# More zero products in the opening chain of an attention and feed-forward kernel, and the last pair of token blocks stored in the ordinary way

## The chip, the cores and the metric

The kernel runs on one core of one Trainium2 chip. The metric is the device time of one execution in microseconds (us). Before the change it is 247.01 us, the median of 8 runs that lie between 246.40 and 247.34 us. Lower is better.

The engines are named as in the profile: PE (TensorE, products), PEld (its weight loads), DVE (VectorE), ACT (ScalarE), POOL (GpSimd) and SP (SyncE, which here only issues transfers). A "q" behind a name (SPq, ACTq) means the engine's instruction queue rather than its arithmetic.

## The reference

For 8 batches, 8 heads, 576 positions and a head width of 64, a 32-slot memory attention is computed and fed to a bilinear feed-forward layer:

```
a      = softmax over the 32 slots of phi
k_m    = a^T k          v_m = a^T v          (32 x 64 per head)
attn   = softmax(q k_m^T / 8)                (576 x 32 per head)
x      = attn v_m, heads put side by side    (4608 x 512)
result = ((x @ w_a) * (x @ w_b)) @ w_out     (512 -> 1536 -> 512)
```

Inputs and result are float32; the kernel computes in float16 with float32 sums.

## The kernel before, in words

**Work per batch.** A batch goes through named units (a dictionary `us[b]` of closures, lines 187 to 382). The ones that matter here: `exp0`, `exp1` take the exponential of phi on ACT (L195); `ks`/`vs` sum k and v under those weights on PE (L256), with a reciprocal and a scaling on DVE (L265, L266); `kt`/`vt` transpose the sums on PE (L274), copied out by DVE (L277); `qt` transposes q on DVE (L204); `s` makes scores on PE (L292); `e` takes their exponential on ACT (L305); `den` sums them on PE (L314), with a logarithm on ACT (L315); `nr` normalises on ACT and DVE (L323, L325). Then `v..`/`hv..` fold v_m into the weights w_a and w_b on PE (L337), and `x..`/`hx..` copy the folded weights out of PSUM on ACT and DVE (L349). A fold needs its columns of w_a or w_b in SBUF: `hv0` columns 0 to 255, `hv1` 256 to 511, `v1` 512 to 1023, `v2` 1024 to 1535; `a` stands for w_a and `b` for w_b.

**Up and down.** `up` (L584) multiplies the attention by the folded weights, one block of 128 feed-forward columns at a time: `pa` (L592), copied by ACT (L595), `pb` (L602), and their product on DVE (L605) into `ht`. `down` multiplies `ht` by w_out, first singly (L389), later for two token blocks at a time in seven products of half size, as Strassen's method does (`two_downs`, L453; its products are L462).

**Loads.** All weights and most inputs are cast from float32 to float16 by transfers that POOL issues in the order of the code (L111 to L176). The order is q, k and v of batch 0, then w_a and w_b in the column pieces named above (`load_wab`, L98 to L100), then w_out in thirds, mixed with batch 1.

**The opening.** PE runs 16 products of a zeroed tile (`fill`, L147; `cols` is the width, 512 in this first call and 256 in the chain). Then `chain(0, ...)` (L671) calls the units of batch 0 in the written order; an entry `f2` in that list is `fill(2, 256)`, two zero products whose result nobody reads. Each `fill` takes one PSUM bank from a list in which the longest unused bank is first (`Banks`, L122). Then `ups` (L672 to L674) runs the first twelve `up` blocks with the folds put between them by an explicit list, one entry after each `pa` and each `pb`. PE does all this in program order. For batch 0 the order is: `hv0a`, `pa` of block 0, `hv0b`, `pb`, `hv1a`, block 1 with `hv1b` behind it, block 2, `v1a`, block 3, `v1b`, blocks 4 and 5, `pa` of block 6, `v2a`, `v2b`, the rest.

**The end.** `two_downs` makes two output tiles of 128 tokens by 512 columns, `o1` and `o2`, in four quarters, in this order: right half of `o1`, right half of `o2`, left half of `o1` (each a DVE addition, L473), left half of `o2` (a scaling). `store` (L447) issues two transfers per tile, one for each 64 tokens. Elsewhere in the kernel a whole tile is stored by two transfers of 128 KB on SP as soon as its last quarter is there. For the last pair (`ends`, L458) each half tile is stored by itself, two transfers of 64 KB each: right `o1` on POOL, POOL (L492); right `o2` on SP, ACT (L498); left `o1` on SP, ACT (L506); left `o2` on SP, ACT (L518). There the last quarter is scaled by DVE (L514) instead of ACT (L516).

Of the kernel before, what the change touches and what calls it, by code (L numbers as in the profile page):

```python
# [11 lines left out]
ALU = mybir.AluOpType  # L12
# [6 lines left out]
def kernel(  # L19
# [11 lines left out]
    nc = tc.nc  # L31
# [3 lines left out]
    d_model, d_ff = moe_w_a.shape  # L35
# [111 lines left out]
    def fill(n, cols=512):  # L147

        pw = banks.tile([P, 512], F32, name="pw")
        for _ in range(n):  # L150
            nc.tensor.matmul(pw[:, :cols], warm[:, :P], warm[:, :cols], start=True, stop=True)
# [267 lines left out]
    NH = d_model // 2  # L419
    w_sums = wpool.tile([P, 4, KH, NH], F16, name="w_sums")  # L420

    def quarter(x, y):
        return wo_sb[:, KH * x:KH * (x + 1), NH * y:NH * (y + 1)]
# [7 lines left out]
    def tokens_of(cidx, x):  # L431
        pair, c = divmod(cidx, NI)
        return ht[:, KH * x:KH * (x + 1), P * c:P * (c + 1)]
# [13 lines left out]
    def store(o_sb, cidx, cs=slice(0, d_model), engines=(nc.sync, nc.sync)):  # L447
        pair, c = divmod(cidx, NI)
        for z in range(2):
            slot = 2 * c + z  # L450
            engines[z].dma_start(out=out_rows[2 * pair + slot // NI, slot % NI, :, cs], in_=o_sb[64 * z:64 * z + 64, cs])

    def two_downs(self, cidx):  # L453
        S1, S2, S4, S3 = (h_sums[cidx][:, x] for x in range(4))
        T1, T2, T3, T4 = (w_sums[:, x] for x in range(4))
        (a11, a12), (a21, a22) = ([tokens_of(cidx + y, x) for x in range(2)] for y in range(2))
        scale = 1.0 / (CS * CS)
        ends = cidx == PAIRED[-1]  # L458

        def products(po, lhs, rhs, first=False):  # L460
            for i in range(KH):
                nc.tensor.matmul(po, lhs[:, i], rhs[:, i], start=first and i == 0,  # L462
                                 stop=i == KH - 1, skip_group_check=not first)
                if i < KH - 1:
                    yield

        def part(po, name):
            x = ppool.tile([P, NH], F32, name=name)
            nc.scalar.mul(out=x, in_=po, mul=scale)  # L469
            return x  # L470

        def plus(o, po, x):
            nc.vector.scalar_tensor_tensor(out=o, in0=po, scalar=scale, in1=x, op0=ALU.mult, op1=ALU.add)  # L473

        o1, o2 = (opool.tile([P, d_model], F32, name="o_sb") for _ in range(2))
        y, ybank = banks.take([P, NH], F32, "py", hold=True)
        yield from products(y, a11, quarter(0, 0), True)
        u1 = part(y, "u1")
        yield
        v, vbank = banks.take([P, NH], F32, "pv", hold=True)  # L480
        self.brim = True
        yield from products(v, S1, T1, True)
        u5 = part(v, "u5")
        yield
        yield from products(y, S2, T2)
        u2 = part(y, "u2")
        yield
        yield from products(v, S4, quarter(1, 1))
        banks.free(vbank)
        plus(o1[:, NH:], v, u2)  # L490
        if ends:
            store(o1, cidx, slice(NH, d_model), (nc.gpsimd, nc.gpsimd))  # L492
        self.brim = False
        yield
        yield from products(y, S3, T3)
        plus(o2[:, NH:], y, u5)
        if ends:
            store(o2, cidx + 1, slice(NH, d_model), (nc.sync, nc.scalar))  # L498
        yield
        x, xbank = banks.take([P, NH], F32, "px", hold=True)  # L500
        self.brim = True
        yield from products(x, a12, quarter(1, 0), True)
        banks.free(xbank)
        plus(o1[:, :NH], x, u1)
        if ends:
            store(o1, cidx, slice(0, NH), (nc.sync, nc.scalar))  # L506
        else:
            store(o1, cidx)
        self.brim = False
        yield  # L510
        yield from products(y, a22, T4)
        banks.free(ybank)
        if ends:
            nc.vector.tensor_scalar(out=o2[:, :NH], in0=y, scalar1=scale, scalar2=None, op0=ALU.mult)  # L514
        else:
            nc.scalar.mul(out=o2[:, :NH], in_=y, mul=scale)  # L516
        if ends:
            store(o2, cidx + 1, slice(0, NH), (nc.sync, nc.scalar))  # L518
        else:
            store(o2, cidx + 1)  # L520
        yield
# [5 lines left out]
    class Work:  # L527
# [10 lines left out]
        def products(self):  # L538
            for cidx in PAIRED:
                yield from two_downs(self, cidx)  # L540
# [67 lines left out]
    def ups(steps, side=()):  # L608

        side = iter(side)  # L610
        for step in steps:
            for _ in up(*step):
                work.advance()
                next(side, us[step[0]]["-"])()
        for f in side:
            work.advance()
            f()

    def steps(b, lo, hi):

        return [(b, i, (0, 1)) for i in range(lo, hi)]
# [14 lines left out]
    def slots(b, names):  # L636

        def both(fs):
            return lambda: [f() for f in fs]
        def unit(n):  # L640
            if n == "fin":
                return lambda: work.pull(-work.done % NFF)
            if n == "L":
                return lambda: load(b + 2) if b + 2 < B else None
            if n[0] == "y":
                return lambda: some(int(n[1:]))
            if n[0] == "d" and n[1:].isdigit():
                return lambda: work.pull(int(n[1:]))
            return us[b + n.endswith("'") - n.endswith("_")][n.rstrip("'_")]

        return [both([unit(n) for n in x.split("+")]) for x in names.split()]
# [3 lines left out]
    def some(n):  # L655
        for _ in range(n):
            next(early, None)

    def chain(b, plan):


        for x in plan.split():
            if x[0] == "f":
                fill(int(x[1:]), 256)
            elif x[0] == "y":
                some(int(x[1:]))
            else:
                us[b][x]()

    fill(16)  # L670
    chain(0, "exp0 exp1 ks0 kt0 qt0 qt1 f2 s0 e0 ks1 kt1 den0 qt2 qt3 f2 s1 nr0 e1 vs0 vs1 den1 vt0 vt1 nr10 nr11 hv0a hx0a")  # L671
    ups(steps(0, 0, 4), slots(0, "hv0b+hx0b hv1a+hx1a - hv1b+hx1b - v1a+x1a - v1b+x1b"))  # L672
    load(2)
    ups(steps(0, 4, 12), slots(0, "- - - - v2a+x2a+v2b+x2b - -"))  # L674
# [48 lines left out]
```

The softmax here doesn't subtract the row's maximum and nothing guards it: scores larger than these inputs give would overflow.

## Time and profile before

| what | value |
|---|---|
| median of 8 runs | 247.01 us |
| the profiled execution's own time | 247.07 us |
| its span (first to last instruction) | 245.3 us |
| PE busy | 231.8 us, 94% of the span |
| PEld, DVE, ACT, POOL busy | 67%, 69%, 64%, 63% |
| granted PE clock, mean | 0.986 |
| chain that ended last: PE, transfers | 82%, 11% |
| `pw` zero products in the chain | 4, of 256 columns |

The profile is a page of one execution and a trace that can be asked for more. Its start times are microseconds from the first instruction. A line of a timeline gives the start, the length, the engine, the source line, the operation with output and inputs, the number of instructions merged into the line, and in brackets the idle time of that engine before it with what ended it. The start of a transfer is its issue; "to landing" counts from there to the moment at which its semaphore tells that the data have arrived. The granted clock (PEclk) is a share of full speed. The lengths of products overlap: 128x288 products start 0.12 us apart at a clock of 1, though each is listed with some 0.29 us.

### The profile page before, as it was taken

What the parts mean: (1) busy time and instruction counts of PE and PEld (TensorE: products, weight loads), DVE (VectorE), ACT (ScalarE), POOL (GpSimd) and SP (SyncE); (2) the same over time, 40 slices, a digit from 0 to 9 for tenths busy, and PEclk for the clock granted to TensorE, in tenths of its full rate; (3) what the DMA queues carried; (4) which work ended last, traced back from release to release, by engine and by line L of the source; (5) the groups of instructions that cost most, each with busy time, mean ns of one, the idle gap of its engine ahead of it and who ended that gap; (6) DMA issues with size and microseconds to landing.
All of it is one profiled execution on the core that took longest, in us unless ns stands there. A gap on an engine that the chain in (4) does not pass through costs nothing.

```text
span 245.3 us, 7629 instructions
## 1 busy us (share of the span) xinstructions
PE 231.8 (94%) x3016; PEld 165.2 (67%) x3016; DVE 168.9 (69%) x406; ACT 158.2 (64%) x409; POOL 153.9 (63%) x126
## 2 busy tenths in 40 slices
PE   7569999999998999999999999999999999999993
PEld 2234574456655857777787777877787877888882
DVE  3454794477959958876995549866996576756742
ACT  2364772678697489578855858577856867565330
POOL 8734263499799028892798769892849177937001
PEclk9995999999999999999999999999999999999999
DMA  6999999999969803983059832597030303032154
GB/s 203 208 197 207 207 256 207 256 217 285 224 179 208 173 2 104 230 142 88 16 130 226 194 86 43 153 198 172 21 68 3 86 3 87 4 87 55 43 128 119
DMA packets 26099, 33.81 MB, mean 138 GB/s; under 512 B 1968, under 2 KB 20528, under 8 KB 26064
## 3 DMA queue, kind: packets, MB, share of 16 engines
q0 software_dynamic: 19344, 22.84, 50.9%
q1 hardware_dynamic: 6208, 9.70, 15.9%
q10 hardware_dynamic: 512, 0.79, 0.9%
q8 instruction: 23, 0.38, 0.6%
q14 instruction: 12, 0.10, 0.1%
HBM read 42.47 MB, written 9.44 MB: 212 GB/s over the span
## 4 chain that ended last, share of the span: by engine, by line
PE 82%; DMA 11%; DVE 3%; issue 1%; ACT 1%; POOL 1%; DVEq 0%; POOLq 0%
PE pa L592 19%; PE pb L602 18%; PE py L462 16%; PE pv L462 8%; DMA wb_sb<-in_moe_w_b_dram 7%; PE pva L337 5%; PE po L389 5%; DMA kv_sb<-in_v_dram 4%; PE px L462 4%; PE pkv L213 2%; PE pD L314 2%; PE pscore L292 1%; PE pT L242 1%; PE pk L256 1%; POOL q_sb L90 1%
## 5 line engine op out<-in xcount | busy, mean ns | idle before, releaser
L605 DVE TENSOR_TENSOR ht<-a_sb,pb 128x288 f16<-128x288 f16 x192 | 83.0, 449 | 42.1 <-ACT a_sb L595 28.7
L595 ACT CAST a_sb<-pa 128x288 f16<-128x288 f32 x192 | 75.1, 405 | 31.7 <-PE pa L592 29.3
L592 PE MATMUL pa<-A,vab 128*128 128x288 f16 x384 | 77.7, 292 | 1.5 <-DVE A L325 1.1
L602 PE MATMUL pb<-A,vab 128*128 128x288 f16 x384 | 77.3, 290 | 0.7 <-ACT vab L349 0.5
L444 POOL TENSOR_TENSOR h_sums<-ht 128x768 f16<-128x768 f16 x28 | 45.8, 1639 | 38.9 <-DVE ht L605 37.3
L602 PEld LDWEIGHTS <-vab 128*128 128x128 f16 x384 | 37.6, 99 | 13.5 <-issue 1.7
L592 PEld LDWEIGHTS <-vab 128*128 128x128 f16 x384 | 34.9, 99 | 16.0 <-issue 8.7
L462 PEld LDWEIGHTS <-h_sums 128*128 128x128 f16 x384 | 37.4, 98 | 6.9 <-issue 0.4
L349 ACT CAST vab<-pva 128x512 f16<-128x512 f32 (+1 forms) x52 | 28.0, 559 | 12.8 <-PE pva L337 12.8
L349 DVE CAST vab<-pva 128x512 f16<-128x512 f32 (+1 forms) x52 | 32.6, 644 | 2.8 <-PE pva L337 2.2
L462 PEld LDWEIGHTS <-ht 128*128 128x128 f16 x288 | 28.2, 98 | 5.6 <-issue 0.4
L462 PE MATMUL py<-w_sums,h_sums 128*128 128x256 f16 x192 | 30.3, 272 | 0.0
L444 POOL TENSOR_TENSOR h_sums<-h_sums,ht 128x768 f16<-128x768 f16 x14 | 23.1, 1649 | 0.9
L444 POOL TENSOR_TENSOR h_sums<-ht,h_sums 128x768 f16<-128x768 f16 x14 | 23.0, 1640 | 1.0
L305 ACT ACTIVATE E<-pscore 128x288 f16<-128x288 f32 x32 | 11.4, 417 | 11.3 <-PE pscore L292 11.2
L325 POOL TENSOR_TENSOR A<-E,R 128x576 f16<-128x576 f16 x10 | 12.7, 1275 | 7.0 <-ACT R L323 6.7
L462 PE MATMUL py<-wo_sb,ht 128*128 128x256 f16 x96 | 16.0, 273 | 0.0
L462 PE MATMUL pv<-w_sums,h_sums 128*128 128x256 f16 x96 | 16.0, 273 | 0.0
L469 ACT ACTIVATE u<-py 128x256 f32<-128x256 f32 x32 | 12.4, 387 | 5.2 <-PE py L462 5.0
L462 PE MATMUL py<-w_sums,ht 128*128 128x256 f16 x96 | 15.5, 272 | 0.1
L462 PE MATMUL px<-wo_sb,ht 128*128 128x256 f16 x96 | 15.4, 273 | 0.0
L204 DVE STREAM_TRANSPOSE qT<-q_sb 128x288 f32<-128x288 f32 x32 | 14.3, 462 | 0.6 <-DMA q_sb<-in_q_dram 0.6
(64 smaller groups left out, 261.1 us busy)
## 6 DMA issues: line engine op xcount, KB each, us to landing
out_dram<-o_sb SPq DMA_DIRECT2D x68, 128.0 KB, 2.8
kv_sb<-in_v_dram POOLq DMA_DIRECT2D x7, 576.0 KB, 10.3
phi_sb<-in_phi_dram POOLq DMA_DIRECT2D x7, 576.0 KB, 4.6
kv_sb<-in_k_dram POOLq DMA_DIRECT2D x7, 576.0 KB, 8.8
q_sb<-in_q_dram POOLq DMA_DIRECT2D x6, 576.0 KB, 13.3
wo_sb<-in_moe_w_out_dram POOLq DMA_DIRECT2D x3, 512.0 KB, 16.3
q_sb<-in_q_dram POOLq DMA_DIRECT2D x4, 288.0 KB, 12.6
wa_sb<-in_moe_w_a_dram POOLq DMA_DIRECT2D x2, 512.0 KB, 14.9
```

Of the source, the lines that this page charges most:

```text
L204: nc.vector.transpose(out=t["qT"][:, hp, :].bitcast(F32), in_=qs[b][:, hp, :].bitcast(F32))
L325: engine.tensor_tensor(out=attn[b][:, g, sl], in0=t["E"][:, g, sl], in1=t["R", g][:, sl], op=ALU.mult)
L337: nc.tensor.matmul(t["pva", lo, z][g][0][32 * j:32 * j + 32, 0:hi - lo], t["kvT"][64 * r:64 * r + 64, 4 + g, M * j:M * j + M], w_sbs[z][64 ...
L349: engine_copy(out=vabs[b][z][:, g, lo:hi], in_=pva[:, 0:hi - lo])
L389: nc.tensor.matmul(po, ht[:, i, P * c:P * (c + 1)], wo_sb[:, i, :], start=(i == 0), stop=(i == NFF - 1))
L444: engine.tensor_tensor(out=out, in0=in0, in1=in1, op=op)
L462: nc.tensor.matmul(po, lhs[:, i], rhs[:, i], start=first and i == 0, stop=i == KH - 1, skip_group_check=not first)
L469: nc.scalar.mul(out=x, in_=po, mul=scale)
L592: nc.tensor.matmul(pa, vab[0][:, g, fs], A[:, g, HALF * hf:HALF * (hf + 1)], start=(g == 0), stop=(g == 1))
L595: nc.scalar.copy(out=a_sb, in_=pa)
L602: nc.tensor.matmul(pb, vab[1][:, g, fs], A[:, g, HALF * hf:HALF * (hf + 1)], start=(g == 0), stop=(g == 1))
L605: nc.vector.tensor_tensor(out=ht[:, i, t0:t0 + HALF], in0=a_sbs[hf - hfs[0]], in1=pb, op=ALU.mult)
```

## The change

Two edits. In the last pair, the stores change: right `o1` is no longer stored by itself; right `o2` goes to SP, SP; `o1` is stored as a whole tile on SP, SP; left `o2` still goes to SP, ACT, and is scaled by ACT. In the chain of batch 0 the two entries `f2` become `f7` and `f5`, and eight further `f` entries are put in: 57 zero products of 256 columns in place of 4.

```diff
         plus(o1[:, NH:], v, u2)
-        if ends:
-            store(o1, cidx, slice(NH, d_model), (nc.gpsimd, nc.gpsimd))
...
         plus(o2[:, NH:], y, u5)
         if ends:
-            store(o2, cidx + 1, slice(NH, d_model), (nc.sync, nc.scalar))
+            store(o2, cidx + 1, slice(NH, d_model))
...
         plus(o1[:, :NH], x, u1)
-        if ends:
-            store(o1, cidx, slice(0, NH), (nc.sync, nc.scalar))
-        else:
-            store(o1, cidx)
+        store(o1, cidx)
...
-        if ends:
-            nc.vector.tensor_scalar(out=o2[:, :NH], in0=y, scalar1=scale, scalar2=None, op0=ALU.mult)
-        else:
-            nc.scalar.mul(out=o2[:, :NH], in_=y, mul=scale)
+        nc.scalar.mul(out=o2[:, :NH], in_=y, mul=scale)
         if ends:
             store(o2, cidx + 1, slice(0, NH), (nc.sync, nc.scalar))
...
-    chain(0, "exp0 exp1 ks0 kt0 qt0 qt1 f2 s0 e0 ks1 kt1 den0 qt2 qt3 f2 s1 nr0 e1 vs0 vs1 den1 vt0 vt1 nr10 nr11 hv0a hx0a")
+    chain(0, "exp0 exp1 f12 ks0 f5 kt0 qt0 qt1 f7 s0 e0 ks1 f5 kt1 f3 den0 qt2 qt3 f5 s1 nr0 e1 f10 vs0 vs1 den1 f3 vt0 vt1 nr10 nr11 f3 hv0a hx0a f4")
```

## The prediction

> **What bounds the kernel now.** The page gives PE 94% of the span, but that is a mean, and the change touches only the two ends. So I read the chain that ended last for the opening, then the table by stage for the clock, then the timeline of PE, then the transfers at the end. The chain, in order of time (start, length, what):
>
> ```profile
> 3.60 10.25 DMA kv_sb<-in_v_dram
> ...
> 14.13 16.32 DMA wb_sb<-in_moe_w_b_dram
> 30.45 0.04 issue
> 30.50 0.41 PE pva L337 x8
> 30.91 0.60 PE pb L602 x4
> ```
>
> Up to 30.45 us the chain is transfers: the fold `v2b` starts 0.04 us after the last piece of w_b lands. From 30.5 on PE works nearly without a hole. The same holds fold by fold. Issue plus time to landing, transfer by transfer, gives the landings of w_a, w_b in pairs: 16.5 and 17.7 (`hv0`), 19.0 and 20.3 (`hv1`), 22.9 and 25.4 (`v1`), 27.9 and 30.4 (`v2`). The folds started at 16.6, 18.9, 20.9, 23.3, 25.2, 26.6, 30.0 and 30.5. PE waited 0.40 us for the last one, so it was early there, though only by that much.
>
> The clock, by stage (start:end, length, busy time of each engine with its instructions, granted clock, transfers):
>
> ```profile
> 4.17:11.00 6.83, 4.45 (x96) 2.18 (x98) 2.39 (x7) 1.50 (x3) 5.69 (x11) 1.00 1.18 252
> 11.00:17.82 6.82, 4.11 (x146) 2.01 (x132) 3.79 (x13) 4.23 (x12) 2.29 (x4) 1.00 1.38 199
> 17.82:24.65 6.83, 6.34 (x45) 3.10 (x46) 2.95 (x8) 3.04 (x8) 2.95 (x4) 0.50 1.26 206
> 24.65:31.47 6.82, 6.58 (x71) 3.68 (x70) 5.45 (x12) 5.14 (x14) 2.10 (x3) 1.00 1.23 222
> ```
>
> After a stretch with PE busy 4.11 of 6.82 us, the next 6.83 us are granted half speed. That is what the zero products can act on. The transfers, second last column, are loaded alike in all four rows.
>
> The timeline of PE shows where it waits in the chain:
>
> ```profile
> 7.58 0.68 PE L256 MATMUL pk<-kv_sb,exp_sb 64*32 64x128 f16 x36 [1.27 <-ACT exp_sb L195]
> 8.85 0.30 PE L274 MATMUL pT<-ident,kvm 128*32 128x128 f16 x8 [0.59 <-DVE kvm L266]
> ...
> 13.89 0.78 PE L256 MATMUL pk<-kv_sb,exp_sb 64*32 64x64 f16 x72
> ...
> 16.50 0.22 PE L274 MATMUL pT<-ident,kvm 128*32 128x128 f16 x1 [1.17 <-issue]
> ```
>
> **The zero products, what they cost.** A 128x288 product steps 0.12 us at full clock, so one of 256 columns steps about 0.11; 53 more of them are 5.8 us of PE. `f12` is 1.3 us against 1.27 idle; each `f5` ahead of a `kt` is 0.55 against 0.59; `f7` is 0.75 against the old `f2` and the 0.46 idle ahead of `s0`: nothing. The first `f3` (0.33) has no hole: `den0` and ACT's work behind it move by 0.33. The second `f5` adds 0.33 ahead of `s1`, whose first hole was 0.21 and whose end hangs on the q transpose on DVE: nothing to 0.1. `f10` (1.1) stands where PE had no hole, at 13.89: `vs` and `den1` move by 1.1. But the last transpose sat until 16.50, as w_a landed at 16.5, so `hv0a` moves only by the `f3` ahead of it, 0.2 to 0.3. `den1`, its logarithm (0.71), exponential (0.78) and product (0.52) end some 0.5 later than 17.41, so the first `pa` starts at 18.0 to 18.3 instead of 17.82, with `f4` in its 0.49 idle. PSUM banks: followed through the list, each zero product takes a bank whose reader ended over 0.5 us before; no wait.
>
> **What they gain.** At full clock, the 21 `pa`/`pb` products of the slow stretch step 0.12 instead of 0.24: 2.5 us. PE would come to `v2b` at 30.50 - 0.40 - 2.5 + 0.5 = 28.1, and then wait 2.4 us for w_b. Transfers don't depend on PE here: w_b was issued at 14.13, after a landing. So the gain at 30.5 is nothing, and the cost too. If the zero products do not hold the clock, the 0.5 us of delay stands against 0.40 of margin: 0.1 us lost. Were w_b early for a reason unseen, the next landings cap the gain: k of batch 1 landed at 37.2 and was used at 38.28, the second third of w_out at 41.2, used at 41.83. That leaves 0.6 us at most. **I take 0**, bounds -0.6 and +0.3.
>
> The Trainium skill, "TensorE: Matmul & The Clock Gate", under "Why this matters for your kernels", asks for no idle gap of PE over about 3 us. The longest gap ahead of the slow stretch was 1.27 us, so here the trace differs: many short gaps and small tiles were enough. By the rule these fills would be idle; by the trace they may hold the clock; the end is the same either way.
>
> **The last stores.** Before, eight half-tile transfers went out on three queues. Now the issues of SP (start, length), the pair before the last with whole tiles, then the last two issues:
>
> ```profile
> 231.69 0.47 SPq L451 DMA_DIRECT2D out_dram<-o_sb  x1
> 232.20 0.60 SPq L451 DMA_DIRECT2D out_dram<-o_sb  x1
> 232.89 0.54 SPq L451 DMA_DIRECT2D out_dram<-o_sb  x1
> 233.48 0.60 SPq L451 DMA_DIRECT2D out_dram<-o_sb  x1
> ...
> 241.74 0.47 SPq L451 DMA_DIRECT2D out_dram<-o_sb  x1
> 241.90 0.55 ACTq L451 DMA_DIRECT2D out_dram<-o_sb  x1
> ```
>
> Back to back, SP's issues start 0.51, 0.69 and 0.59 us apart. After the change SP has five from 240.41 (right `o2` is ready then, as before): 240.41 and 240.92 for right `o2`, 241.61 and 242.20 for `o1` (ready at 241.03, so it queues), and the first half of left `o2` at 242.89. Before, SP issued that at 241.74 and ACT the other at 241.90. The last issue is thus 0.99 later. Time to landing was 2.2 us for both last issues and 2.2 to 2.4 for whole tiles; from the last landing (241.90 + 2.2 = 244.1) to the end of the span (245.3) it was 1.2. New span: 242.89 + 2.2 + 1.2 = 246.3, **+1.0 us**. Bounds: issues 0.52 apart (0.47 plus the gap of 0.05) and a landing of 2.0 give 242.49 + 2.0 + 1.2 = 245.7, +0.4; 0.69 apart and the slowest landing of this end, 2.9, give 243.17 + 2.9 + 1.2 = 247.3, +2.0. I take the SP rhythm of the pair before, the same sequence of tiles.
>
> ACT scales the last quarter in 0.38 us, DVE took 0.42; ACT's previous work ended at 239.04, so nothing is queued and its store goes out near 241.7, landing near 243.9, ahead of SP's. The two POOL stores that vanish ended their issue at 241.21 and were not last: nothing gained.
>
> The Trainium skill, "DMA: Bandwidth & Descriptors", "Rules for kernel authors", speaks against my sum: spreading transfers over queues gives no bandwidth, it saves only issue time. By the first half this edit costs 0; by the second the whole issue time of SP. The trace has no store of three queues merged into one, but SP's rhythm above is issue time.
>
> **Sum.** The profiled execution took 247.07 us, 0.06 above the median; 247.07 + 0 + 1.0 = **248.0 us**.
>
> **Rivals.**
> 1. *The opening pays (not slower).* The margin at `v2b` is 0.40 us with the slow stretch at 17.82. In executions where this stretch starts over 0.4 us later against the landings, PE misses w_b, and holding the clock earns it back. For it: that margin is small, and the runs spread over 0.94 us. Against: the profiled execution lost nothing there and is still above the median. The lowest run bounds the price: 247.01 - 246.40 = 0.6 gained, so 247.4, within 0.2% of before. Chance 0.13.
> 2. *The tail is hidden, the opening pays.* Issue at the low bound, +0.4, and 1.0 gained: 246.4, faster. Against it: the landings at 37.2 and 41.2. Chance 0.06.
> 3. *The clock falls later.* PE idles some 2.5 us (ahead of `v1b`, `v2a`, `v2b`) in the stretch 24.65:31.47 if it runs at full clock before, which leaves about 4.1 of 6.8 us busy, as in the stretch that was followed by half clock. Then 31.47 to 38.3, where PE has no hole, would lose 3.4 us: 251.4. Against: the first row above was busy 4.45 us without a fall, 2.5 of it full 128-row zero products; the second had 1.2 us of full-size work; here there would be over 3 us of `pa` and `pb`. Chance 0.07.
> 4. *The zero products do not hold the clock* (the change doesn't do what it says): +0.1, 248.1, inside the forecast.
>
> **How the numbers follow.** The forecast with rival 4 has 0.74: 247.5 to 248.9 by the bounds of the tail and the opening that I hold likely. About 0.2% is what a measurement of this kernel can tell from no change, here 246.5 to 247.5. The range, 247.2 to 248.9, takes in rival 1; rivals 2 and 3 and the ends of the bounds are left out. Slower 0.79 (the forecast 0.72, rival 3 0.07), same 0.15 (rival 1 and the low end of the tail), faster 0.06.
>
> **What would show it.** After the change: granted clock 1.00 at 17.8 to 24.7, `v2b` still some 0.04 us after the landing of w_b at about 30.45, PE idle ahead of it over 1 us; five SP issues from 240.4 to 243.4, the last landing near 245.1, a span of 246.3. I am wrong if w_b lands earlier, if SP issues faster than 0.5 us apart, or if the clock reads 0.50 anywhere after 31 us.

## The result and the profile after

The changed kernel takes **247.96 us** (median of 11 runs, 247.39 to 248.27), the kernel before 247.0 (median of 32 runs). The ratio is 1.0037, with a 95% interval of 1.0029 to 1.0046: slower by 0.7 to 1.1 us. The forecast was 248.0. The profiled execution after took 247.62 us, with a span of 245.9 us, 0.3 below its median; that of before was close to its own. Single executions of four of the kernels below lie 3 to 6 us above the others at a lower mean clock than most; the times given leave them out. Line numbers after the change are 8 lower behind the edit: `pa` is L584, `pb` L594, the scaling on ACT L508.

The end first. These are SP's five issues in the timeline of the changed kernel (start, length):

```profile
240.27 0.47 SPq L451 DMA_DIRECT2D out_dram<-o_sb  x1
240.78 0.60 SPq L451 DMA_DIRECT2D out_dram<-o_sb  x1
241.48 0.54 SPq L451 DMA_DIRECT2D out_dram<-o_sb  x1
242.06 0.60 SPq L451 DMA_DIRECT2D out_dram<-o_sb  x1
242.76 0.55 SPq L451 DMA_DIRECT2D out_dram<-o_sb  x1
```

The distances are 0.51, 0.70, 0.58 and 0.70, those of the pair before the last within 0.01. PE's last product starts at 240.84 here and at 240.97 in the kernel before, so measured from there the last issue went from +0.92 to +1.92: 1.00 us later, as worked out. ACT's store, issued at 241.56, landed at 244.07; SP's last one landed at 244.76. All of the kernel behind PE's last product took 4.37 us before and 5.07 after.

Now the opening. The table by stage has the same columns as before, with stretches cut as in the prediction:

```profile
4.17:11.00 6.83, 6.83 (x80) 3.90 (x79) 2.39 (x7) 1.26 (x2) 5.60 (x11) 1.00 1.18 252
11.00:17.82 6.82, 5.84 (x174) 4.07 (x174) 2.42 (x8) 2.71 (x7) 2.46 (x5) 1.00 1.38 199
17.82:24.65 6.83, 6.18 (x75) 3.18 (x73) 4.14 (x13) 4.77 (x14) 2.88 (x4) 1.00 1.26 206
24.65:31.47 6.82, 6.38 (x69) 3.58 (x68) 5.79 (x13) 4.86 (x12) 2.12 (x3) 1.00 1.23 222
```

No stretch is at half clock any more. In the third one PE starts 24 `pa` and `pb` products and 32 of the folds, where it had started 21 and 24; of the 75 in the row another 10 are zero products. Still, the chain that ended last goes through the same transfer as before:

```profile
14.22 16.08 DMA wb_sb<-in_moe_w_b_dram
30.29 0.04 issue
30.34 0.41 PE pva L337 x8
30.75 0.60 PE pb L594 x4
```

PE was ready earlier and waited. The timeline says so in the bracket of the last fold:

```profile
29.63 0.41 PE L337 MATMUL pva<-wa_sb,kvT 64*32 64x512 f16 x8
30.34 0.41 PE L337 MATMUL pva<-wb_sb,kvT 64*32 64x512 f16 x8 [0.29 <-DMA wb_sb<-in_moe_w_b_dram]
```

That wait is a good deal shorter than the 2.4 us of the prediction. The reason is in PE's timeline of the chain:

```profile
1.26 7.13 PE L151 MATMUL pw<-warm 128*128 128x512 f16 x28 [1.26 <-DVE warm L120]
8.32 0.68 PE L256 MATMUL pk<-kv_sb,exp_sb 64*32 64x128 f16 x36
...
13.26 0.41 PE L314 MATMUL pD<-E,ones 128*128 128x288 f16 x2
...
17.12 0.44 PE L256 MATMUL pk<-kv_sb,exp_sb 64*32 64x64 f16 x34 [0.94 <-issue]
...
19.65 0.82 PE L584 MATMUL pa<-A,vab 128*128 128x288 f16 x4
```

The first sums start at 8.32 instead of 7.58, and the first `pa` at 19.65 instead of 17.82. From there to the fold `v2a` it takes 9.98 us instead of 12.17. So this stretch, at full clock throughout, is 2.2 us shorter, the chain ahead of it 1.8 us longer, and `v2a` only 0.36 us earlier.

### The profile page after: what moved, and what is told of

Read it like the earlier page. It is cut to its first block, busy times and chain, and to the rows that moved or that the text cites. A ratio compares the mean times of both kernels' runs of the same rounds, so it can differ in the third digit from the quotient of the medians.

```text
span 245.9 us, 7731 instructions
## 1 busy us (share of the span) xinstructions
PE 235.4 (96%) x3069; PEld 168.8 (69%) x3069; DVE 168.4 (68%) x405; ACT 158.2 (64%) x410; POOL 152.9 (62%) x124
## 4 chain that ended last, share of the span: by engine, by line
PE 82%; DMA 11%; DVE 3%; issue 1%; ACT 1%; POOL 1%; DVEq 0%; POOLq 0%
PE pa L584 19%; PE pb L594 18%; PE py L462 16%; PE pv L462 8%; DMA wb_sb<-in_moe_w_b_dram 7%; PE pva L337 5%; PE po L389 5%; DMA kv_sb<-in_v_dram 4%; PE px L462 4%; PE pkv L213 2%; PE pD L314 2%; PE pscore L292 1%; PE pT L242 1%; PE pk L256 1%; POOL q_sb L90 1%
## 5 line engine op out<-in xcount | busy, mean ns | idle before, releaser
L584 PE MATMUL pa<-A,vab 128*128 128x288 f16 x384 | 76.5, 287 | 1.1 <-DVE A L325 1.1
L594 PE MATMUL pb<-A,vab 128*128 128x288 f16 x384 | 76.4, 286 | 0.8 <-ACT vab L349 0.6
L594 PEld LDWEIGHTS <-vab 128*128 128x128 f16 x384 | 37.0, 98 | 13.4 <-issue 1.7
L584 PEld LDWEIGHTS <-vab 128*128 128x128 f16 x384 | 34.5, 98 | 15.2 <-issue 8.3
L462 PE MATMUL py<-w_sums,h_sums 128*128 128x256 f16 x192 | 30.3, 272 | 0.0
L325 POOL TENSOR_TENSOR A<-E,R 128x576 f16<-128x576 f16 x10 | 12.7, 1275 | 7.0 <-ACT R L323 6.8
L315 ACT ACTIVATE L<-pD 128x288 f32<-128x288 f32 x32 | 11.5, 418 | 5.8 <-PE pD L314 5.5
```

Source lines behind the costliest of these rows:

```text
L315: nc.scalar.activation(out=t["L", g][:, sl], in_=pD, func=AF.Ln)
L325: engine.tensor_tensor(out=attn[b][:, g, sl], in0=t["E"][:, g, sl], in1=t["R", g][:, sl], op=ALU.mult)
L584: nc.tensor.matmul(pa, vab[0][:, g, fs], A[:, g, HALF * hf:HALF * (hf + 1)], start=(g == 0), stop=(g == 1))
L594: nc.tensor.matmul(pb, vab[1][:, g, fs], A[:, g, HALF * hf:HALF * (hf + 1)], start=(g == 0), stop=(g == 1))
```

## The experiments

Two theories stood against each other. The **SP theory**: all of the loss is the issue time of five transfers in a row on SP, and the fills are hidden behind the landing of w_b. The **fills theory**: the fills pay a part of it. A third, that the later and larger store of `o1` costs by itself, came up for the end of the kernel.

### The two edits one by one

The kernel before with the zero products and the old stores (the line of the chain from the change, alone; chain lines are cut short with dots here):

```diff
-    chain(0, "exp0 exp1 ks0 kt0 qt0 qt1 f2 ...
+    chain(0, "exp0 exp1 f12 ks0 f5 kt0 qt0 qt1 f7 ...
```

> The 53 added zero products with the old last stores. SP theory (all of the +0.96 us is the five issues in a row on SP, the fills are hidden behind the landing of w_b): 247.0 us, ratio 1.000 within 0.001. Fills theory (they delay the opening, which pays part of the +0.96): 247.3 to 247.9.

Measured: 247.12 us, ratio 1.0009 (1.0000 to 1.0019), so 0 to 0.5 us of loss. The changed kernel with the old chain (that line put back):

```diff
-    chain(0, "exp0 exp1 f12 ks0 f5 kt0 qt0 qt1 f7 ...
+    chain(0, "exp0 exp1 ks0 kt0 qt0 qt1 f2 ...
```

> The new last stores with the old chain of batch 0. SP theory: 247.96 us, ratio 1.004. Fills theory: what the first kernel of this set does not show, 247.1 to 247.7.

Measured: 247.7 us, ratio 1.0030 (1.0018 to 1.0041), so 0.44 to 1.0 us. From PE's last product to the end it took 5.06 us, the kernel with the fills alone 4.36. By the medians the stores make 0.75 us of the 0.96, by the interval half of it or all. For the fills both theories stay possible: 0.17 us by the medians, with an interval that touches zero.

### Which part of the stores

In the changed kernel SP's five issues are taken down to three, by moving the whole-tile `o1` to POOL:

```diff
-        store(o1, cidx)
+        store(o1, cidx, engines=(nc.gpsimd, nc.gpsimd) if ends else (nc.sync, nc.sync))
```

> The changed kernel, but the whole-tile o1 of the last pair is stored by POOL, POOL instead of SP, SP, so SP has three issues in place of five. The bytes and the moment at which o1 is ready stay as changed. SP theory: last SP issue some 1.2 us earlier, 247.0 us (246.9 to 247.3). Rival (the later, larger store of o1 itself is the cost, on whatever queue): 247.7 to 248.0.

Measured: 248.30 us, ratio 1.0059 (1.0045 to 1.0074). Neither theory had that: it is slower than with five issues on SP. The timeline, and then the landings of the last three issues from its view of the output (least, median, most):

```profile
241.35 1.17 POOL L451 DMA_DIRECT2D out_dram<-o_sb  x2 [15.91 <-DVE o_sb L473]
241.72 0.55 ACTq L451 DMA_DIRECT2D out_dram<-o_sb  x1
```

```profile
DMA to landing us min/median/max: 2.3/3.0/3.4
```

The last issue is at 241.94, 0.94 behind PE's last product, as early as in the kernel before. But POOL begins 0.29 us after DVE is done with `o1` (SP begins 0.03 after), its second half lands after 3.0 us, and the ACT store issued beside it after 3.4 us, where the last two of the kernel before had 2.2; SP's took 2.3. So the issue time is not the whole story of an end: with 256 KB on POOL's queue in the last 5 us, two of the last three stores landed about 1 us later. What held them is not shown.

A smaller step in the changed kernel was to take one issue from SP:

```diff
-            store(o2, cidx + 1, slice(NH, d_model))
+            store(o2, cidx + 1, slice(NH, d_model), (nc.sync, nc.scalar))
```

> The changed kernel, but right o2 goes to SP, ACT as before, so SP has four issues in place of five. SP theory: one issue of 0.6 us less, 247.4 us (247.2 to 247.5), half way back. Rival (late and larger o1): no change from 247.96.

Measured: 247.5 us, ratio 1.0025 (1.0015 to 1.0035). The last issue came 1.28 behind PE's last product, in place of 1.92, and the end 4.73 in place of 5.07. One issue less is worth 0.64 us at the issue; nearly half of that is lost again as the last landing took 2.29 instead of 2.0.

The opposite edit takes the kernel before, keeps its half-tile transfers, and makes five issues in a row on SP:

```diff
         plus(o2[:, NH:], y, u5)
-            store(o2, cidx + 1, slice(NH, d_model), (nc.sync, nc.scalar))
+            store(o2, cidx + 1, slice(NH, d_model))
         plus(o1[:, :NH], x, u1)
-            store(o1, cidx, slice(0, NH), (nc.sync, nc.scalar))
+            store(o1, cidx, slice(0, NH))
```

> The kernel before with five issues in a row on SP in the last pair, but its half-tile transfers kept: right o1 on POOL, POOL; right o2 on SP, SP; left o1 on SP, SP; left o2 on SP, ACT. The late bytes are those of before, only the queue is that of the change. If SP's issue time alone sets the end: last SP issue 1.0 us later, 247.8 us (247.6 to 248.0). If the late whole tile matters as much (the run with o1 on POOL had few SP issues and was still 1.4 slower): 247.3 to 247.5. If only the late bytes matter: 247.0.

Measured: 247.67 us, ratio 1.0026 (1.0016 to 1.0035), the same as the new stores alone. The last issue:

```profile
242.74 0.54 SPq L451 DMA_DIRECT2D out_dram<-o_sb  x1
```

It comes 1.92 behind PE's last product, and the end 5.07 behind it, the same two numbers as after the change. So the late whole tile on SP costs nothing that shows beside this; the five issues in a row do it.

An attempt at a faster end than both kernels starts from the kernel before: the last store of ACT no longer behind another one, and the last quarter scaled by two engines.

```diff
-            store(o1, cidx, slice(0, NH), (nc.sync, nc.scalar))
+            store(o1, cidx, slice(0, NH), (nc.sync, nc.gpsimd))
...
-            nc.vector.tensor_scalar(out=o2[:, :NH], in0=y, scalar1=scale, scalar2=None, op0=ALU.mult)
+            nc.vector.tensor_scalar(out=o2[:, :P], in0=y[:, :P], scalar1=scale, scalar2=None, op0=ALU.mult)
+            nc.scalar.mul(out=o2[:, P:NH], in_=y[:, P:], mul=scale)
```

> The kernel before with left o1 stored by SP, POOL (ACT is then free for the last store, whose issue had waited for the one before until 241.90) and the last quarter scaled half by DVE and half by ACT. 0.16 us for the earlier issue and about 0.13 for the shorter scaling: 246.7 us, ratio 0.9988. If POOL's slower issue or landing becomes the end: 247.0 or above.

Measured: 246.98 us, ratio 0.9998 (0.9986 to 1.0010): no gain. ACT did not work beside DVE but after it (the bracket names what it waited for; DVE's half ended at 241.41):

```profile
241.44 0.28 ACT L515 ACTIVATE o_sb<-py 128x128 f32<-128x128 f32 x1 [2.56 <-DVE o_sb L514]
241.75 0.50 ACTq L451 DMA_DIRECT2D out_dram<-o_sb  x1
```

0.30 + 0.28 in a row is longer than the 0.42 of one engine, which eats what the freed queue gave. The version shows nothing about two engines at once. No kernel here that computes the same result is faster than the kernel before.

### Does the landing of w_b gate the opening?

The kernel before with no zero products in the chain at all (the two `f2` taken out):

```diff
-    chain(0, "exp0 exp1 ks0 kt0 qt0 qt1 f2 s0 ... qt2 qt3 f2 s1 ...
+    chain(0, "exp0 exp1 ks0 kt0 qt0 qt1 s0 ... qt2 qt3 s1 ...
```

> The kernel before without its 4 zero products in the chain. Gate theory: still 247.0 us, within 0.3, whatever the clock does. Rival (the clock in the opening decides): half clock comes earlier or lasts longer, 247.5 to 249.

Measured: 247.01 us, ratio 0.9999 (0.9990 to 1.0007). Its table by stage:

```profile
7.15:10.55 3.40, 1.96 (x58) 1.03 (x61) 1.62 (x6) 0.87 (x2) 3.12 (x6) 1.00 1.21 206
10.56:24.20 13.64, 11.64 (x208) 5.28 (x195) 6.45 (x20) 7.06 (x19) 5.62 (x8) 0.50 1.32 202
```

Half clock for 13.6 us, twice as long as before, and not 0.2 us of time: the last fold started at 30.42, 0.04 after w_b landed. This alone is a weak test of the gate, though, as PE came to `v2a` at 29.91, no later than the 29.99 of before: the half clock ended 0.4 us sooner, and the 1.17 us wait at 16.50 is not in this profile.

Stronger is what the other profiles show. In two of them, the changed kernel with `o1` on POOL and with four issues on SP, PE came to `v2a` over 1 us earlier. The first:

```profile
28.85 0.41 PE L337 MATMUL pva<-wa_sb,kvT 64*32 64x512 f16 x8
30.53 0.41 PE L337 MATMUL pva<-wb_sb,kvT 64*32 64x512 f16 x8 [1.26 <-DMA wb_sb<-in_moe_w_b_dram]
```

The next fold waited for the landing all the same. In eight of the nine profiles with all loads and up to 57 zero products the last fold started 0.04 or 0.05 us after w_b landed, whenever between 28.85 and 30.02 PE had come to `v2a`. In the ninth, the kernel before with five issues on SP, PE came at 30.13 and the last fold was 0.19 behind the landing. The kernel before shows the same without an edit: of its 77 runs recorded beside the experiments, the 15 with a mean clock of 1.000 have a median of 246.92 us, the others 247.0.

The other way round, the changed kernel with 30 more zero products ahead of the first sums:

```diff
-    chain(0, "exp0 exp1 f12 ks0 ...
+    chain(0, "exp0 exp1 f42 ks0 ...
```

> The changed kernel with 30 further zero products ahead of the first sums (f42 for f12), 30 x 0.11 = 3.3 us of PE. If the landing of w_b at 30.3 us gates the opening and PE waits for it by 0.3 to 0.6 us as in the profile of the changed kernel, all above that is lost: 3.3 - 0.6 = 2.7, 250.6 us (250.2 to 251.0). By the margin of 2.4 us that the prediction worked out: 3.3 - 2.4 = 0.9, 248.9. Were fills free anywhere: 248.0.

Measured: 253.2 us, ratio 1.0240 (1.0208 to 1.0271), 5.2 us above the changed kernel. The last fold started at 32.8 in place of 30.3: 2.4 us lost there and 0.9 of the 3.3 hidden. Not all of the 0.9 is the margin ahead of w_b, as the 0.94 us stop of PE at 17.12 is not in this profile either. The rest of the loss came later. The six runs fall into two groups, 252.0 to 252.3 and 254.1 to 254.4 us, and the profile is of the slower one. In it, in batch 1, DVE's product of attention and reciprocal (`A`, L325) took 4.24 us; the kernel before has

```profile
48.27 0.45 DVE L325 TENSOR_TENSOR A<-E,R 128x576 f16<-128x576 f16 x1
```

To see what the fills are worth where nothing hides them, the last third of w_a and w_b was left out of the kernel before (two transfers that write 512 KB each, about 5 us by an estimate from the 206 GB/s of the table), so that the result is another one:

```diff
-    load_wab(1024, 1536)
...
-                            w_sbs[z][64 * r:64 * r + 64, hp, lo:hi],
+                            w_sbs[z][64 * r:64 * r + 64, hp, lo % 1024:lo % 1024 + hi - lo],
```

> The kernel before, with the last third of w_a and w_b not loaded (the fold of columns 1024 to 1535 takes columns 0 to 511 instead, so the result is another one). Some 5 us of transfers are gone and nothing gates the last fold. By the profile PE was ready for it at 30.1 where it started at 30.5: 0.4 us faster, 246.6 us. If transfers and not PE bound the opening by far: 244 to 245.

> The same lightened kernel with the 53 added zero products (old last stores). It shows what the fills do where no landing covers them. By the two profiles (ready for the last fold at 29.7 with them, at 30.1 without): 0.4 us faster than the lightened kernel without them, 246.2 us. By the prediction's working (2.5 gained on the clock, 0.5 paid): 2.0 faster, 244.6. If fills cost more than the clock gives: 247 or above.

Measured: 248.69 us (ratio 1.0088, 1.0058 to 1.0119) and, with the fills, 250.08 us (1.0129, 1.0112 to 1.0145). With less to load the kernel is slower, which no theory had. At the opening the two profiles are as expected: the last fold at 29.93, with the fills at 29.34. Then both ran into the long `A`. DVE, then POOL, in the lightened kernel without fills:

```profile
47.69 4.24 DVE L324 TENSOR_TENSOR A<-E,R 128x576 f16<-128x576 f16 x1
```

```profile
47.01 0.74 POOL L85 DMA_DIRECT2D kv_sb<-in_v_dram  x1 [5.02 <-PE pk L255]
47.74 0.75 POOL L90 DMA_DIRECT2D q_sb<-in_q_dram  x1
48.50 3.10 POOL L428 TENSOR_TENSOR w_sums<-wo_sb 128x1536 f16<-128x1536 f16 x1
```

`A` begins at the end of one load issue of POOL, and ends at 51.93, 0.33 us after POOL's first sum of w_out ends. In the kernel before `A` started at 48.27, and POOL went on so:

```profile
48.63 0.74 POOL L90 DMA_DIRECT2D q_sb<-in_q_dram  x1 [0.29 <-DVE kvT L277]
49.39 3.11 POOL L429 TENSOR_TENSOR w_sums<-wo_sb 128x1536 f16<-128x1536 f16 x1
```

There the issue began 0.36 us after `A`, and the sum 1.1 us after `A`; in the lightened kernel 0.05 and 0.8. The Trainium skill, "SBUF — State Buffer", "Who interferes with whom", states that a DVE instruction with two inputs in SBUF contends with a GpSimd instruction that reads SBUF, that the ports they share are an exclusive lock, and that the order of issue decides which of them is blocked. The long `A` fits the lock; that it was held by a sum listed as starting 0.36 us after `A` would have been done does not follow from the rule.

The test, in the lightened kernel without and with the fills: POOL's sums are made to wait until `A` is done, by a copy of one of its columns:

```diff
     load(3)
+    gap = consts.tile([P, 1], F16, name="gap")
+    nc.gpsimd.tensor_copy(out=gap, in_=attn[1][:, 1, 0:1])
     sum_weights()
```

> The lightened kernel (last third of w_a, w_b not loaded, other result), and POOL copies one column of the attention of batch 1 ahead of its w_out sums, so that these can't start before DVE's product of that attention is done. In the lightened kernel that product took 4.24 us in place of 0.45, from POOL's issue of a load to the end of its first w_out sum. If that collision is what made it 2 us slower: the product back to 0.5 to 1.2 us, and 246.4 us (its last fold started 0.6 earlier than in the kernel before). If the lighter load itself does harm: 249.0 as without the copy.

> The same with the 53 added zero products: what they are worth where no landing covers them. Last fold 0.6 us earlier than in the lightened kernel without them, as their two profiles show: 245.8 us, 0.6 below it. By the prediction's working (2.5 gained, 0.5 paid): 2.0 below. If the fills only cost: above it.

Measured: 246.58 us (ratio 0.9973, 0.9953 to 0.9993) and 246.59 us (0.9980, 0.9966 to 0.9994). In the kernel without fills:

```profile
49.33 0.45 DVE L324 TENSOR_TENSOR A<-E,R 128x576 f16<-128x576 f16 x1
```

It begins beside the same two issues of POOL as in the lightened kernel (48.66 and 49.39 here), so it was the sum and not the issue that held it. With the collision 2.1 us are gone by the medians, and 3.5 with the fills.

The 0.6 us that the fills were expected to gain here did not come: between these two kernels they make no difference in the median. The last folds of two profiles were too little to go by. In these two kernels, whose opening is that of the two lightened ones, it came at 31.57 and 30.39, over 1 us later than there. The fills do make a difference in the spread: without them the 12 runs lie between 244.73 us (mean clock 0.998) and 248.19 (0.977), with them between 245.66 and 247.26, with a mean clock of 0.998 to 1.000 in all. Without them the three runs with a mean clock of 0.993 or more took 244.73 to 245.67 us, the seven of 0.983 or less 246.49 to 248.19. So where no landing covers the opening, a held clock goes with shorter runs, and the fills seem to cost about what they save.

## Why the prediction was right, and where its working was off

**The opening gives nothing: right, and the landing of w_b is why.** PE came to `v2a` up to 1 us earlier or not, at full clock or half, and the last fold stayed with the landing of w_b. Of the two bounds, -0.6 to +0.3, the measured 0 to +0.5 lies at the upper end and a little beyond. A loss of some 0.2 us by the fills is neither shown nor excluded: w_b landed at 30.29 to 30.66 in the five profiles with them, at 30.17 to 30.45 in five without, and there is one more block of PE's instructions fetched before 30 us with them. That this is the cause was not tried.

**The reading of the folds was too wide.** "The same holds fold by fold" does not fit the prediction's own numbers: only the last fold started at its landing. `hv0a` came 0.2 us after its own by coincidence (below), and the others 1.2 to 3 us after theirs, when PE's order brought them up. The forecast needed the last one alone.

**The working inside the opening was off.** "The first `pa` starts at 18.0 to 18.3": it started at 19.65. Three things were missing. `f12` was priced at full clock, but PE's first products start 0.43 us apart until 5.75 us in this execution and 0.22 after, though the row from 4.17 on reads 1.00 (in the one before the distances change at 4.2). So the products ahead of the sums took 0.7 us more. The wait at 16.50 was put down to w_a landing at 16.5, by a coincidence of times. After the change w_a landed at 15.27, and PE still stopped until 17.12. The stop goes with the fetching of instructions (below), it does not stay at that place, and so it did not swallow `f10`. And the delays add, as PE works in program order. The margin ahead of the last fold was 0.3 us by the bracket in this execution (0.5 counted from the 0.23 us that one fold takes after another) and 1.3 to 1.4 by the bracket in the profiles of the two kernels whose clock came up at 4.0 and 4.6 us; not 2.4. The sign "PE idle ahead of it over 1 us" thus failed in this execution, with the forecast unharmed.

**The stores cost 1.0: right in the place, 0.25 to 0.3 us too high.** The issue moved by 1.00 as worked out. The last landing took 2.0 instead of 2.2, and the rest behind it 1.15 instead of 1.22, so the end moved by 0.70 in the traces; by the medians of the stores alone 0.75, with an interval of 0.44 to 1.0. That the sum was right to 0.04 us is partly luck: this excess was made up by some 0.2 us that the sum does not have, by the medians a cost of the fills.

**ACT for the last quarter, POOL's stores gone: nothing, as forecast.** ACT scaled at 241.15 and its store was not the last.

**The rivals.** For the rival that the opening pays nothing was found: the fills alone were not faster. That the clock falls later did not happen in this kernel (0.995 to 1.000 in all 11 runs), but the lightened kernel with fills and the one with 30 more did fall to half clock for 3.4 us, when PE stood idle behind the long `A`.

**The rule against the stores.** That queues share their transfer engines fits the run with `o1` on POOL, where the ACT store beside it landed late, but was not tested by itself. That several queues save only issue time fits the loss on SP: the last issue came 1.00 us later, and the end 0.70.

## What to carry to other kernels

Before speeding up an engine in a stage, look at which landing ends that stage: here the clock could be halved for 13.6 us, or held, with at most some tenths of a microsecond to show for it. At the end of a kernel count the issues in each queue behind the last product: on SP each costs 0.5 to 0.7 us. Look at the landings too: with a large store moved to POOL, two of the last three took 3.0 and 3.4 us. And a step moved by a few us can meet another engine's work elsewhere; look at the longest single instruction of a group, not at its mean.

## What the runs showed of the hardware

**PE seems to have stopped for its own instructions.** In the kernel before and after, the wait with "issue" as its cause (1.17 us at 16.50, 0.94 us at 17.12) comes behind exactly 223 products, in different lines of the program. In both, a 16 KB packet on the queue q8, which carries instructions (taken here to be PE's), ended 1.3 us before PE went on (15.17 to 16.50, 15.80 to 17.12). Twelve of the fourteen traces have this stop, all behind 223 products and 1.3 to 1.5 us after that packet. In the other two, the one without fills and the one with 30 more, PE came to this place 2.0 and 2.6 us after the packet and did not stop. No run was made to test it. The page after counts these blocks:

```profile
q8 instruction: 24, 0.39, 0.6%
```

That is 16 KB each, and one more than before. The Trainium skill, "Runtime: NRT & Kernel Launch", "Instruction fetch mechanics", gives blocks of 16 KiB, 256 instructions each, which agrees with the packets, and calls the crossing mostly hidden; here, if this reading is right, PE stood idle there for 0.7 to 1.7 us.

**Zero products do hold the clock.** With 57 of them the mean granted clock was 0.995 or more in every run of the changed kernel; with none it was half for 13.6 us, though no gap of PE in the chain was over 0.8 us by the brackets.

**A 0.45 us product on DVE took 4.24 us** in the three profiles where POOL's sum of two SBUF tiles is listed 0.81 us after its start. In the others the sum came 0.93 to 1.29 us after it, and the product took 0.45. Why a sum that is listed so much later holds it stays open.
